# A stored sequence of steps in place of a planner's due times, in a kernel of attention and two feed-forward stages

## The chip, the cores and the metric

The kernel runs on one core of one Trainium2 chip. Times are microseconds (us) that the device takes for one execution, unless marked ns. The engines have short names here: PE is TensorE (matmuls), DVE is VectorE, ACT is ScalarE, POOL is GpSimd, and SP is SyncE, which issues all the DMAs of this kernel.

## What is computed

The reference has three stages in a row, on 4 batches of 576 tokens:

```python
scores = scale * q @ k.T                     # 4 batches, 8 heads, 576 x 64
# heads 0-3: a window of 32 tokens; heads 4-7: 128 tokens, every fourth
x = softmax(where(mask, scores, -1e9)) @ v   # as 2304 tokens x 512
h = x @ w_in                                 # 512 -> 1024
s = h * softmax(h)
x = (s - mean(s)) / sqrt(var(s) + 1e-6) * g_ln @ w_out    # 1024 -> 512
h = x @ w2_in                                # 512 -> 2048
out = softplus(h) @ w2_out                   # 2048 -> 512
```

Everything is float32 in and out. The kernel gets near float32 by splitting operands into a high and a low float16 part and adding three float16 products.

## The kernel before

The function describes its work as some 2,700 **steps**. A step has a name, the engines on which it may run (some can run on either ACT or DVE), a function that issues its instructions, the steps that must be over before it, and the buffers it uses, each from a pool with a few slots. There are 417 steps on PE, 343 on SP (the DMAs), and the rest are on ACT and DVE. Then `Plan.order` brings all steps into one sequence, and the last loop of the function issues them in that order, each on the engine that the plan gave it. An engine runs its instructions in the order in which they were issued, so this sequence is the whole schedule.

The names that come up below, in the order of the work:

- `ldN`, `pre..`, `w1i`, `w1o`, `w2i0` to `w2o3`: loads of a pair of attention blocks, the passes that find the scale of a batch, and the preparation of the weights in quarters (convert on DVE, square on ACT, a small matmul `...m` on PE that sums the squares, then a high half and a low half).
- `tqN`, `tkN`, `QKN`, `tpN`, `PVN`, `txN`: transposes, scores and values of attention pair N on PE. Pairs 0 to 9 are in float32 and use PE's transposes; pairs 10 to 27 are in float16 and use DMA transposes (`qT`, `kT`, `pT`, `xT`). With them go `cq`, `ck`, `cp`, `kh`, `ph`, `nr`, `xh` on ACT or DVE.
- `m1aT`, `m1bT`: the first matmul for token tile T (two steps of 12 matmuls); `m1n`, `m1h` and others are its normalisation.
- `yaJ`, `ybJ`: the matmul with `w_out` for a group J of 256 tokens.
- `hJ.P`, `oJ.P`: the last two matmuls (24 matmuls of 256 columns, 12 of 512); `sp`, `gh`, `gl` are softplus and the split between them. Groups 5 to 8 are done in pairs with seven products for eight, `P5..` and `P7..`.

`Plan.order` of the kernel before is a list scheduler. It keeps a clock of its own, a price for each step, and a latest time for each (`TABLE`, one number per step, in tenths of a us). Whenever an engine is free it takes the ready step with the earliest latest time whose buffers can be had, in the first free slot of each pool. A step that may run on either engine carries 509.77 us more on DVE's list (`SHY`). A step that needs ACT's other function table carries 20 us (`CLING`). When PE is free and has nothing ready in the first 400 us, the plan puts in a **fill**: one 128x512 matmul of the identity into a free PSUM slot, whose result nobody reads.

```python
            free = [f for f in self.fills if not f[0][0]]
            if idle_at["PE"] <= now + 1e-9 and now < self.FILL_END and free:
                idle_at["PE"] = self.pace(now, *self.FILL)
                ...
                out.append(min(free, key=lambda f: f[0][1])[1])
```

The sequence that comes out has 417 PE steps and 163 fills, 540 steps on ACT and 1,392 on DVE. ACT changes its table 53 times in it.

## Time and profile before

| | us |
|---|---|
| three runs | 704.28, 704.89, 707.59 |
| median | 704.89 |
| the profiled execution | 705.82 |
| its span, from the first to the last instruction | 704.1 |
| PE busy in the span | 680.0 |
| DVE busy | 569.9 |
| ACT busy | 464.7 |

### The profile page before, as it was taken

To read this page: it belongs to the slowest core of one execution; us is meant where nothing else is said; L and a number is where in the kernel's file an instruction comes from. 1 tells how busy PE (TensorE), PEld (TensorE's weight loads), DVE (VectorE), ACT (ScalarE), POOL (GpSimd) and SP (SyncE) were. 2 spreads that over 40 slices of the span, in tenths; PEclk is the share of its full clock that TensorE was granted. 3 is DMA by queue.
4 is the path that set the end of the run, shared out by engine and by line. 5 is a ranking of instruction groups with operands and counts; after the bars stand their busy time and mean duration, and the time that the engine had idled before them with its cause. 6 is when DMAs were issued, how large, how long until landed. Compare 5 with 4: busy or idle time off the path is not lost.

```text
span 704.1 us, 14232 instructions
## 1 busy us (share of the span) xinstructions
PE 680.0 (97%) x5244; PEld 465.6 (66%) x5244; DVE 569.9 (81%) x1668; ACT 464.7 (66%) x946; POOL 3.5 (1%) x22
## 2 busy tenths in 40 slices
PE   5999798999999999999999999999999999999997
PEld 3665556867766477778657767665867768777543
DVE  4799999999999887788989999898996487445342
ACT  5597997998977586778978878856655325123100
POOL 2000000000000000000000000000000000000000
PEclk9999779999999999999999999999999999999999
DMA  9977886669785448979887877453021110001001
GB/s 275 269 212 240 232 224 163 172 153 195 155 169 149 141 142 205 217 164 171 156 167 152 155 143 132 94 116 58 8 54 31 31 31 1 1 1 61 1 1 60
DMA packets 186773, 89.80 MB, mean 128 GB/s; under 512 B 157000, under 2 KB 174416, under 8 KB 186704
## 3 DMA queue, kind: packets, MB, share of 16 engines
q1 hardware_dynamic: 186704, 88.90, 54.4%
q8 instruction: 41, 0.67, 0.4%
q14 instruction: 28, 0.23, 0.1%
HBM read 54.53 MB, written 4.72 MB: 84 GB/s over the span
## 4 chain that ended last, share of the span: by engine, by line
PE 72%; DVE 13%; DMA 7%; ACT 4%; issue 2%; SPq 1%; ACTq 0%; DVEq 0%
PE ps_w L680 33%; PE bank L680 27%; PE bank L1678 10%; DVE W L671 2%; PE bank L686 2%; DMA pT<-p 2%; DVE E L671 1%; DMA rk<-in_k_dram 1%; DVE s L1250 1%; DVE st L1376 1%; DMA lnT<-hl 1%; DMA kT<-qk 1%; DVE qk L671 1%; SPq L689 1%; DMA W<-in_moe_w_out_dram 1%
## 5 line engine op out<-in xcount | busy, mean ns | idle before, releaser
L680 PE MATMUL ps_w<-W,g 128*128 128x512 f16 x864 | 194.2, 379 | 0.0
L680 PEld LDWEIGHTS <-W 128*128 128x128 f16 x1824 | 176.6, 98 | 24.9 <-issue 2.4
L680 PEld LDWEIGHTS <-g 128*128 128x128 f16 x864 | 83.3, 98 | 92.1
L680 PE MATMUL bank<-y,W 128*128 128x256 f16 x960 | 110.1, 273 | 1.6 <-ACT r L662 1.6
L680 PE MATMUL ps_w<-W,xr 128*128 128x512 f16 x432 | 99.5, 383 | 0.3 <-ACT xr L662 0.3
L680 PE MATMUL bank<-lnT,W 128*128 128x256 f16 x864 | 98.7, 273 | 0.0
L680 PEld LDWEIGHTS <-xr 128*128 128x128 f16 x432 | 41.9, 99 | 46.6 <-issue 2.0
L1853 ACT ACT_TABLE_LOAD x53 | 68.0, 1283 | 0.9
L662 ACT ACTIVATE s<-s 96x128 f32<-96x128 f32 (+3 forms) x144 | 43.8, 375 | 13.4 <-DVE s L668 11.8
L1678 PEld LDWEIGHTS <-W 128*128 128x128 f16 x480 | 46.9, 98 | 7.6
L671 DVE SCALAR_TENSOR_TENSOR g<-r,KR,g 128x512 f16<-128x512 f32 x66 | 49.2, 746 | 2.5 <-ACT g L662 0.4
L662 ACT ACTIVATE E<-E 128x768 f32<-128x768 f32 (+2 forms) x49 | 36.4, 744 | 14.8 <-DVE st L671 3.7
L666 DVE TENSOR_SCALAR g<-r,KR 128x512 f16<-128x512 f32 x35 | 16.9, 482 | 33.2 <-PE ps_w L680 30.1
L1250 DVE CUSTOM_DVE_ANT_0 s<-bank,band,bsc 96x128 f32<-96x128 f32 (+3 forms) x144 | 38.9, 322 | 1.3 <-PE bank L680 0.6
L662 ACT ACTIVATE r<-r,invT 128x512 f32<-128x512 f32 x19 | 13.4, 718 | 32.8 <-DVE r L674 32.8
L662 ACT ACTIVATE hl<-e,st 128x1024 f16<-128x1024 f32 x18 | 22.2, 1235 | 12.6 <-DMA lnT<-hl 8.2
L662 ACT ACTIVATE r<-bank,invC 128x512 f32<-128x512 f32 x40 | 27.3, 682 | 2.4 <-PE bank L680 1.6
L680 PEld LDWEIGHTS <-eye 128*128 128x128 bf16 (+2 forms) x183 | 18.4, 107 | 15.0 <-issue 4.1
L680 PEld LDWEIGHTS <-pT 128*96 128x96 f16 (+3 forms) x432 | 23.1, 124 | 7.2 <-DMA pT<-p 2.9
L662 ACT ACTIVATE e<-ps_w,st,bsc 128x1024 f32<-128x1024 f32 x16 | 19.3, 1205 | 11.6 <-DVE rs L666 4.5
L680 PE MATMUL ps_w<-eye 128*128 128x512 bf16 x101 | 26.9, 379 | 0.0
L671 DVE SCALAR_TENSOR_TENSOR E<-E 128x512 int32<-128x512 int32 x40 | 26.4, 681 | 0.1
(293 smaller groups left out, 1114.0 us busy)
## 6 DMA issues: line engine op xcount, KB each, us to landing
E<-in_moe_w_in_dram SPq DMA_DIRECT2D x17, 512.0 KB, 5.1
E<-in_moe_w_out_dram SPq DMA_DIRECT2D x17, 512.0 KB, 4.4
out_dram<-osb SPq DMA_DIRECT2D x18, 256.0 KB, 2.2
W<-in_moe_w_in_dram SPq DMA_DIRECT2D x7, 512.0 KB, 7.4
W<-in_moe_w_out_dram SPq DMA_DIRECT2D x7, 512.0 KB, 5.1
E<-in_v_dram SPq DMA_DIRECT2D x9, 384.0 KB, 3.8
E<-in_q_dram SPq DMA_DIRECT2D x9, 384.0 KB, 3.8
E<-in_k_dram SPq DMA_DIRECT2D x9, 384.0 KB, 4.1
```

The lines of the kernel that those rows point to most:

```text
L662: pin(nc.scalar.activation(out=out, in_=in_, func=func, **kw))
L666: pin(nc.vector.tensor_scalar(out=out, in0=in0, scalar1=s1, scalar2=None, op0=op0))
L671: pin(nc.vector.scalar_tensor_tensor(out=out, in0=in0, scalar=s, in1=in1, op0=op0, op1=op1, **kw))
L680: pin(nc.tensor.matmul(out, l, r, start=start, stop=stop))
L686: pin(nc.tensor.transpose(out, in_, eye32[:in_.shape[0], :in_.shape[0]]))
L689: pin(nc.sync.dma_start(out=out, in_=in_))
L1250: pin(nc.vector.tensor_tensor_reduce(out=sv()[:rows, h, :nk], in0=sb.t[:rows, h, :nk], in1=band[:rows, 48 - m:48 - m + nk], scale=sc[:rows ...
L1376: ({"DVE": (1.142, 0.14)}, lambda e: pin(nc.vector.tensor_reduce(out=col(0), in_=ph(), axis=AXX, op=ALU.max, negate=True)), [mb], [ps]),
L1678: pin(nc.tensor.matmul(ps.t[:, ff, :], at(w, cc, ff), yo.t[:, v, cc, :], start=start, stop=cc == 1 and x == 2, skip_group_check=True,))
L1853: pin(nc.scalar.preload_act_table_set(TABLES[tab]))
```

## The change

The steps, their functions, buffers and dependences stay as they are. The list scheduler, its prices and the table of latest times go. In their place stand two stored lists. `ORDER` names the steps one after the other; a number below zero is a fill, and a number at or above the count of steps (2,692) means that the step runs on DVE where it could also run on ACT. `SLOTS` names the slot for each buffer, in the order in which the buffers are first used. `order` only reads them and asserts that dependences and slots are kept:

```diff
-    SHY = 509.77
-    WIN, KEEP, HOLD = 3.4133, 3.0, 3.2
-    FILL = (0.235, 0.48)
...
-    CLING = 20.0
...
     def order(self):
 
-        for o in reversed(self.ops):
-            late = min((s.late for s in o.succ), default=1e9)
...
+        out, over, n = [], set(), len(self.ops)
+        slots = iter(self.slots)
+        for x in self.stored:
+            if x < 0:
+                place, bank = self.fills[-1 - x]
+                assert not place[0]
+                out.append(bank)
+                continue
+            o = self.ops[x % n]
+            assert o not in over and all(a in over for a in o.after), o.name
+            o.on = next(iter(o.opts)) if len(o.opts) == 1 else "DVE" if x >= n else "ACT"
             for b in o.uses:
...
+                if b.slot is None:
+                    assert not b.pool.fifo or b.n == b.pool.next, o.name
+                    b.slot = b.pool.slots[next(slots)]
...
-    TABLE = (
...
+    ORDER = (
+        65, 66, 247, 248, 278, 277, 0, 13, -2, -2, -2, 250, 252, 2943, 3, 2945, 14, 67, 69, -2, -2, 280, 254, 281,
+        1, 255, 266, 267, 256, 15, 16, 4, 249, 68, -5, -5, -5, -5, -5, -5, -5, 257, 5, 279, 282, 6, 28, 308, 18,
...
+    SLOTS = (
+        0, 0, 0, 1, 1, 0, 0, 0, 1, 0, 1, 0, 0, 1, 0, 0, 1, 2, 1, 0, 0, 1, 0, 1, 0, 2, 0, 3, 0, 0, 0, 1, 0, 1, 0, 0,
...
-    lanes = Pool("lanes", [None] * P.LANES, fifo=False)
```

Set beside the sequence before, the stored one holds:

| | before | stored |
|---|---|---|
| fills | 163 | 142 |
| steps on ACT | 540 | 588 |
| steps on DVE | 1,392 | 1,344 |
| changes of ACT's table | 53 | 43 |
| steps that change from DVE to ACT, from ACT to DVE | | 109, 61 |
| PE steps at another place in PE's own order | | 264 of 417 |
| DMAs at another place in SP's own order | | 285 of 343 |

Where the fills stand, and the PE steps around them, at the places that come up later (`[6F]` is six fills):

```
before  [18 fills so far] tk1 [7F] tq1 pre0m ...            58 fills ahead of w1im, 95 of m1a0
        tp8.1 [6F] PV7.0 PV7.1 PV8.0 PV8.1 [7F] tx7.0 [4F] tx7.1 [7F] tx8.0 [3F] ya0.1     133 ahead of ya0.1
        w2i3m [4F] PV13.0 [1F] ... m1b6 m1a7 m1b7 [12F] m1a8 w2o3m m1b8                    163
stored  [3F] tq0 tk0 ... tp0.0 tk1 tp0.1 ...                58 fills ahead of w1im, 88 of m1a0
        tp8.0 [5F] PV7.0 PV7.1 tp8.1 [4F] tx7.0 [6F] tx7.1 PV8.0 PV8.1 [2F] ya0.1          113 ahead of ya0.1
        [1F] w2i3m [3F] PV13.0 [1F] ... [1F] ... m1b6 m1a7 m1b7 [4F] m1a8 w2o3m m1b8       142
```

After `m1a8` neither sequence has a fill.

## Rows read from the trace of the kernel before

**Rows 1.** The page: busy time by engine.

```profile
PE 680.0 (97%) x5244; PEld 465.6 (66%) x5244; DVE 569.9 (81%) x1668; ACT 464.7 (66%) x946; POOL 3.5 (1%) x22
```

**Rows 2.** Windows by stage: stretch, its length, busy time (instructions), clock, DMA.

```profile
0.00:35.20 35.20, 28.04 (x199) 16.72 (x200) 21.14 (x54) 19.91 (x62) 3.52 (x22) 0.95 0.97 272
35.20:134.30 99.10, 91.73 (x693) 61.34 (x692) 97.23 (x283) 88.25 (x255) 0.00 (x0) 0.91 0.72 207
134.30:222.80 88.50, 88.13 (x713) 62.48 (x711) 88.09 (x283) 79.91 (x159) 0.00 (x0) 1.00 0.80 167
222.80:243.90 21.10, 20.82 (x116) 9.89 (x115) 19.54 (x47) 10.18 (x18) 0.00 (x0) 1.00 0.51 150
243.90:456.50 212.60, 208.27 (x1824) 152.45 (x1824) 184.88 (x673) 174.71 (x313) 0.00 (x0) 1.00 0.77 158
456.50:699.40 242.90, 242.90 (x1709) 162.76 (x1707) 158.25 (x333) 91.10 (x142) 0.00 (x0) 1.00 0.14 31
```

**Rows 3.** Timeline of PE: fills at either clock, an early wait; start, length, what.

```profile
11.02 2.54 PE L680 MATMUL bank<-eye 128*128 128x512 bf16 x11
...
16.34 0.47 PE L686 MATMUL bank<-eye,rk 80*128 80x80 f32 x4 [2.77 <-DMA rk<-in_k_dram]
...
87.29 2.34 PE L680 MATMUL bank<-eye 128*128 128x512 bf16 x5
...
238.61 2.75 PE L680 MATMUL bank<-eye 128*128 128x512 bf16 x12
```

**Rows 4.** Lines by form: kinds that move, and the table load.

```profile
L1853 ACT ACT_TABLE_LOAD x53 | 68.0, 1283 | 0.9
...
L662 ACT ACTIVATE xf<-bank,rs 80x64 f32<-80x64 f32 x52 | 11.9, 313 | 2.1 <-DVE rs L677 2.1
...
L1376 DVE TENSOR_REDUCE st<-ps_w 128x1 f32<-128x1024 f32 x18 | 21.9, 1217 | 1.8 <-PE ps_w L680 1.8
...
L662 ACT ACTIVATE e<-e,st 128x1024 f32<-128x1024 f32 x8 | 9.9, 1233 | 1.2 <-DVE st L668 1.1
...
L668 DVE TENSOR_SCALAR e<-e,st 128x1024 f32<-128x1024 f32 x10 | 8.1, 809 | 0.2
...
L674 DVE TENSOR_TENSOR xf<-bank,rs 80x256 f32<-80x256 f32 x19 | 7.9, 417 | 0.2
```

**Rows 5.** Timeline of DVE at 198 us: starts and lengths of neighbours.

```profile
198.26 0.74 DVE L666 TENSOR_SCALAR osb<-ps_w,invD 128x512 f32<-128x512 f32 x1
198.92 0.14 DVE L668 TENSOR_SCALAR s2o<-s2o 128x1 int32<-128x1 int32 x1
```

**Rows 6.** Waits of PE from 243.9 us on: total, times, longest.

```profile
PE bank L680 <- DMA pT<-p: 1.9, 2, 1.5
PE bank L680 <- ACT r L662: 1.2, 2, 0.9
PE bank L680 <- DMA kT<-qk: 0.8, 1, 0.8
PE bank L680 <- DVE s L1250: 0.4, 1, 0.4
```

**Rows 7.** Timeline at the end.

```profile
699.63 0.69 ACT L662 ACTIVATE osb<-ps_w,iD 128x512 f32<-128x512 f32 x1 [4.49 <-PE ps_w L680]
700.36 0.75 DVE L666 TENSOR_SCALAR osb<-ps_w,iD 128x512 f32<-128x512 f32 x1 [4.43 <-ACT osb L662]
```

**Rows 8.** Windows around the stretch in which PE's clock falls.

```profile
74.00:78.00 4.00, 2.12 (x32) 1.84 (x28) 4.00 (x11) 4.00 (x12) 0.00 (x0) 1.00 0.76 250
78.00:94.00 16.00, 13.46 (x69) 9.25 (x70) 15.26 (x39) 16.00 (x45) 0.00 (x0) 0.50 0.95 252
94.00:98.00 4.00, 3.29 (x18) 1.57 (x17) 4.00 (x18) 4.00 (x15) 0.00 (x0) 0.85 1.13 295
```

**Rows 9.** Timeline of PE: a block of 12 matmuls at the low clock, and at the full one.

```profile
92.46 4.11 PE L680 MATMUL ps_w<-W,xr 128*128 128x512 f16 x12
...
241.29 2.75 PE L680 MATMUL ps_w<-W,xr 128*128 128x512 f16 x12
```

## The prediction

> **What bounds the kernel now.** I read the page first. PE is busy 97% of the span [rows 1], but that counts fills and the tails of overlapping matmuls, so it doesn't say where time can be won. The windows by stage do [rows 2]. The last column groups to look at are PE, DVE and ACT against the length of each stretch.

> - To 35.2 us the first pairs and weights come in. No engine is full (PE 28.04 of 35.20, and most of that is fills); the DMA engines are at 0.97 of their share.
> - From 35.2 to 222.8 us DVE is full: 97.23 of 99.10 and 88.09 of 88.50, which leaves 2.3 us idle in 187.6. In the first of these stretches PE is not short of time, since a good part of its 91.73 is fills. In the second PE is full too (88.13), nearly without fills.
> - From 222.8 to 243.9 PE spends 16 fills, 12 of them in a row [rows 3], until the last weight quarter is ready.
> - From 243.9 to 456.5 PE waits only 4.3 us (208.27 of 212.60), and from there to 699.4 not at all (242.90 of 242.90). The last 4.7 us are the last copies and the output.

> So the end is the moment at which the last weight quarter's sum of squares, `w2o3m` at 243.9, goes through, plus a fixed mass of matmuls, plus 4.3 us of waits, plus 4.7. What the change is worth is read from two places: how much earlier `w2o3m` comes, for which DVE's queue is the measure, and how many of the 4.3 us go.

> **DVE's queue ahead of `w2o3m`.** I set the two sequences beside each other and took the steps that stand on DVE up to the last one on which `w2o3m` depends: 593 before, 579 in the stored one. The difference is made of four parts, priced by [rows 4].

> - 20 steps leave for ACT: two `m1n` at 0.809 us, and 18 others of which the commonest is `nr` at 0.417. 2 x 0.809 + 18 x 0.417 = 9.1 us less.
> - 7 steps come from ACT, among them three copies out of PSUM. Bounds: 7 x 0.417 = 2.9, or, at the 0.74 of a 128x512 step out of PSUM [rows 5], 5.2. I take 3.8, nearer to the first because the copies have 320 columns and not 512.
> - The maximum of token tile 7 (1.217) with its small follower goes behind: 1.3 us less. A small step (0.2) comes ahead.

> That is -9.1 + 3.8 - 1.3 + 0.2 = -6.4. But neighbours on DVE overlap: a step of 0.74 us is followed by the next after 0.66 [rows 5]. 14 steps fewer are 14 such overlaps of 0.08 fewer, 1.1 us. Net **-5.3 us**. The same count at `h0.0` (134.3 us) gives -4.7, so most of it is won in the first of DVE's full stretches.

> **The fills say the same.** 21 fills fewer: 12 in a row took 2.75 us and 11 took 2.54 [rows 3], 0.21 each, so 4.4 us. At the low clock five took 2.34, near 0.45 each, which would make 9.4. Fills stand where the planner expected PE to wait, so a shorter wait and fewer fills are one gain and not two. 4.4 and 5.3 agree; I take 5.3, as the measure of the engine that is full, and keep 9.4 as the far end and nothing as the near end.

> **What I cost at nothing.**

> - ACT's extra work ahead of `w2o3m`: five more `nr` net, each four instructions of 0.313, make 6.3; two `m1n` at 1.233 make 2.5; six short steps net at about 0.5 make 3. With overlaps that is some 9 us. It hides in ACT's idle time, 8.6 us in the second full stretch and 10.9 in the one behind it [rows 2]. Without that cover it is a rival below.
> - 10 table loads fewer, 12.8 us of ACT at 1.283 each [rows 4]. Both sequences have 10 changes of table ahead of `w2o3m`, so all ten are saved later, where ACT is busy 174.71 of 212.60 and 91.10 of 242.90 [rows 2]. No gain; if ACT set PE's pace there, up to 1.2 us of waits hang on ACT [rows 6].
> - SP's order. The k load of pair 1 goes from 11th to 4th place, which ends a wait of 2.77 us [rows 3]; the last piece of `w_in` goes from 20th to 24th, behind four more loads of 128 KB, which at 272 GB/s [rows 2] is 1.9 us. Both lie ahead of `w1im`, which has 58 fills before it in either sequence. I take them as cancelling, and keep -2.8 and +1.9 as bounds.
> - Slots. They choose among buffers of equal speed; a bad choice would show as a wait and belongs to the rivals.
> - The end. In both sequences the last `o` is followed by one copy on ACT, one on DVE behind it [rows 7], and the output. 4.7 us stay.

> **The 4.3 us of late waits** are six [rows 6]. Two are for DMA transposes of the probabilities (1.9 us, ahead of `PV19.0` and `PV24.0`), which DVE feeds. By the stored sequence DVE has 13.0 and 14.2 us less ahead of these, and PE 7.8 and 5.6 less: DVE gains on PE by 5.2 and 8.6, more than the 1.5 and 0.4 waited. They go: **-1.9 us**. The other four (2.4 us) keep their distance and stay.

> **Sum.** 704.1 - 5.3 - 1.9 = 696.9 us of span. The profiled execution was 705.82, 1.7 more than its span, and 0.9 above the median of 704.89. I take the 7.2 off the median: **697.7 us**.

> **Rivals.**

> - *ACT becomes the bound* (the other side). Place: 134.3 to 222.8. ACT is busy 79.91 of 88.50 there [rows 2]; ten steps come over to it inside the stretch and none leave, 6.8 us by the kinds above, which makes 86.7. If ACT's 8.6 us of waiting are for the same inputs as before and stay, the stretch takes 95.3, 6.8 more. Should ACT (0.5 us more ahead of `h0.0`) also hold back the 4.7 won until there, the end is 704.89 + 6.8 + 0.5 - 1.9 = 710.3. It decides for slower once more than 3.7 us of the 8.6 stay. For it: ACT is then the fuller engine. Against it: these waits were mostly for DVE's results, and DVE comes earlier; and 12 fills (2.75) behind it are cover. Chance 0.10, of which 0.07 end above 708.4.
> - *PE's clock falls more often.* [...] Chance 0.08, half to each end. [...]
> - *New late waits.* From 456.5 on PE has nothing to win and its order is changed all the same. In the first set of seven products the third was the seventh step of PE behind the seventh product and is now the fourth, with two additions on DVE to be done between. If the stored sequence fits the plan's times closer than the chip's, the 4.3 us of waits double instead of shrinking: 704.89 - 5.3 + 4.3 = 703.9. For it: 264 of 417 PE steps stand elsewhere. Against it: DVE has 10 to 20 us less ahead of PE from 400 us on. Chance 0.10.
> - *The fills were only cover.* PE waits as long as before with fewer fills in the gap; only the 1.9 come: 703.0. For it: ahead of `ya0.1` the fills fall from 133 to 113, while DVE's queue ahead of it, counted as above, does not shrink. Chance 0.06.
> - More than forecast: waits under low-clock fills go too (9.4) and the early 2.8: below 691.5, chance 0.04.

> **How the numbers follow.** The forecast has 0.62, with a range of its own of 692 to 701. From 691.5 to 705 leaves out the 0.04 below and about 0.11 above. A difference under 0.5% (3.5 us) can hardly be told from no change. Faster: 0.62 + 0.04 + 0.04 (the clock's near end) = 0.70. Slower: 0.07 + 0.04 = 0.11. The same: 0.10 + 0.06 + 0.03 = 0.19.

> **What would show it.** Right: `w2o3m` near 238.6 us, the run of fills ahead of it 4 and not 12; DVE still full from 35 to about 218; late waits near 2.4 us with those for DMA `pT` gone; 43 table loads less one or none; 4.7 us at the end. Wrong: ACT full and DVE idle between 130 and 218 (the first rival); more than 16 us of granted clock at 0.50 (the second); waits of PE after 456 us (the third); `w2o3m` still at 243 with gaps in place of fills (the fourth).

## The result, and the profile after

The changed kernel takes 697.87 us (median of 4 runs, 697.51 to 698.44), beside 705.78 for the kernel before in 4 runs of the same session: a ratio of 0.9888, interval 0.986 to 0.9915. The forecast was 697.7 us. The profiled execution took 698.44, its span 696.5.

The page's busy line of the changed kernel, to be set against [rows 1]:

```profile
PE 675.2 (97%) x5223; PEld 463.9 (67%) x5223; DVE 556.0 (80%) x1619; ACT 480.9 (69%) x1015; POOL 3.5 (1%) x22
```

Its windows between the same steps as in [rows 2] (columns as there; `h0.0` now starts at 128.5, `w2i3m` at 218.3, `w2o3m` at 238.2):

```profile
0.00:32.10 32.10, 27.89 (x201) 17.14 (x202) 22.18 (x56) 19.27 (x63) 3.54 (x22) 1.00 0.91 255
32.10:128.50 96.40, 87.84 (x673) 59.21 (x672) 92.47 (x268) 88.07 (x257) 0.00 (x0) 0.91 0.86 222
128.50:218.30 89.80, 89.30 (x716) 62.75 (x715) 88.77 (x284) 86.25 (x179) 0.00 (x0) 1.00 0.78 172
218.30:238.20 19.90, 18.89 (x108) 9.23 (x108) 18.62 (x43) 11.93 (x26) 0.00 (x0) 1.00 0.52 146
238.20:448.80 210.60, 208.08 (x1826) 152.66 (x1825) 179.08 (x649) 176.20 (x341) 0.00 (x0) 1.00 0.80 160
448.80:691.80 243.00, 243.00 (x1709) 162.95 (x1707) 154.17 (x322) 98.50 (x155) 0.00 (x0) 1.00 0.14 31
```

Up to `w2o3m` DVE is busy for 22.18 + 92.47 + 88.77 + 18.62 = 222.0 us, which leaves 16.2 idle. Before it was 226.0 of 243.9, 17.9 idle [rows 2]. So the 5.7 us by which `w2o3m` comes earlier are 4.0 of work and 1.7 of idle time. ACT is busy 86.25 of 89.80 in the third stretch and DVE is still full there; the stretch itself is 1.3 us longer than before. Behind 448.8 nothing has changed: 243.00 of 243.00.

The run of fills ahead of the last weight quarter, in PE's timeline (start, length, what): four, where [rows 3] had twelve.

```profile
234.79 1.03 PE L552 MATMUL bank<-eye 128*128 128x512 bf16 x4
235.66 2.75 PE L552 MATMUL ps_w<-W,xr 128*128 128x512 f16 x12
```

PE's waits from 238.2 us on, the counterpart of [rows 6] (total, times, longest). They sum to 2.4 us, as forecast, but are not the four that were to be left:

```profile
PE bank L552 <- DMA pT<-p: 1.0, 1, 1.0
PE bank L552 <- DMA qT<-qk: 0.5, 1, 0.5
PE bank L552 <- DVE xf L546: 0.5, 1, 0.5
PE bank L552 <- ACT xf L534: 0.4, 1, 0.4
```

So the two profiles put the gain of 7.6 us of span (704.1 to 696.5) in two places: 5.7 ahead of `w2o3m` and 1.9 behind it, where 460.2 us became 458.3 and the waits of PE fell from 4.3 to 2.4.

The table load among the lines by form, ten fewer than in [rows 4], and the end of the timeline, which answers to [rows 7] (696.5 - 691.8 is again 4.7):

```profile
L1718 ACT ACT_TABLE_LOAD x43 | 55.2, 1283 | 0.7
```

```profile
692.04 0.69 ACT L534 ACTIVATE osb<-ps_w,iD 128x512 f32<-128x512 f32 x1 [8.95 <-issue]
...
692.76 0.75 DVE L538 TENSOR_SCALAR osb<-ps_w,iD 128x512 f32<-128x512 f32 x1 [6.69 <-ACT osb L534]
```

PE's clock, in windows of 4 us (compare [rows 8]). The drop to 0.50 comes at about 75 us instead of 78 and lasts no longer, about 17 us in either. In the window ahead of it PE had 2.11 us of work in 4, and in the one in which it comes 0.98:

```profile
70.00:74.00 4.00, 2.11 (x28) 1.65 (x24) 4.00 (x12) 4.00 (x13) 0.00 (x0) 1.00 0.90 276
74.00:78.00 4.00, 0.98 (x9) 0.84 (x9) 4.00 (x10) 2.84 (x8) 0.00 (x0) 0.69 0.98 238
78.00:82.00 4.00, 3.11 (x21) 2.72 (x20) 2.80 (x8) 4.00 (x13) 0.00 (x0) 0.50 0.73 212
...
90.00:94.00 4.00, 4.00 (x18) 1.97 (x16) 3.81 (x13) 4.00 (x10) 0.00 (x0) 0.67 0.99 289
```

Where the lead arises is seen from the starts of PE's steps: `m1a0` 53.6 before and 48.9 after, `h0.0` 134.3 and 128.5, `w2i3m` 222.8 and 218.3, `w2o3m` 243.9 and 238.2, the last `o` 696.8 and 689.2. Of the early lead 3.1 us are there where the second window begins (32.1 for 35.2), and 4.8 at `m1a0`, early in the first stretch in which DVE was full.

### The profile page after: what moved, and what is told of

It is laid out like the page before. It is cut to its first block, busy times and chain, and to the rows that moved or that the text cites. A ratio compares the mean times of both kernels' runs of the same rounds, so it can differ in the third digit from the quotient of the medians.

```text
span 696.5 us, 14184 instructions
## 1 busy us (share of the span) xinstructions
PE 675.2 (97%) x5223; PEld 463.9 (67%) x5223; DVE 556.0 (80%) x1619; ACT 480.9 (69%) x1015; POOL 3.5 (1%) x22
## 2 busy tenths in 40 slices
DMA packets 186773, 89.80 MB, mean 129 GB/s; under 512 B 157000, under 2 KB 174416, under 8 KB 186704
## 4 chain that ended last, share of the span: by engine, by line
PE 69%; DVE 12%; DMA 10%; ACT 4%; issue 3%; SPq 1%; ACTq 0%; DVEq 0%
PE ps_w L552 31%; PE bank L552 26%; PE bank L1550 11%; DMA xd<-x 2%; DVE E L543 2%; DMA E<-in_v_dram 2%; DMA qT<-qk 1%; DMA pT<-p 1%; DVE W L543 1%; PE bank L558 1%; DVE s L1122 1%; DMA W<-in_moe_w_out_dram 1%; ACT E L534 1%; DMA rv<-in_v_dram 1%; DMA rq<-in_q_dram 1%
## 5 line engine op out<-in xcount | busy, mean ns | idle before, releaser
L543 DVE SCALAR_TENSOR_TENSOR g<-r,KR,g 128x512 f16<-128x512 f32 x68 | 50.3, 744 | 15.2 <-ACT g L534 14.2
L534 ACT ACTIVATE E<-E 128x768 f32<-128x768 f32 (+3 forms) x51 | 37.9, 744 | 15.7 <-DVE E L543 8.8
L534 ACT ACTIVATE xf<-bank,rs 80x64 f32<-80x64 f32 (+1 forms) x128 | 29.3, 314 | 7.2 <-DVE rs L549 4.8
L552 PE MATMUL ps_w<-eye 128*128 128x512 bf16 x108 | 31.4, 407 | 0.7 <-DVE e L543 0.7
L534 ACT ACTIVATE g<-r,KR 128x512 f16<-128x512 f32 x35 | 24.9, 715 | 6.6 <-PE ps_w L552 6.3
L552 PEld LDWEIGHTS <-eye 128*128 128x128 bf16 (+2 forms) x162 | 16.5, 111 | 15.8 <-POOL eye L611 4.0
```

The costliest lines, as they stand in the source:

```text
L534: pin(nc.scalar.activation(out=out, in_=in_, func=func, **kw))
L543: pin(nc.vector.scalar_tensor_tensor(out=out, in0=in0, scalar=s, in1=in1, op0=op0, op1=op1, **kw))
L552: pin(nc.tensor.matmul(out, l, r, start=start, stop=stop))
```

## The experiments

Each was timed beside the kernel before, which had a median of 704.84, 704.47 and 705.03 us in the three sessions (e1 to e4, e5 to e8, e9 to e12). Three kinds of edit were made: sequences cut at a step (the one list up to it, the steps that are left in the order of the other), engines put back (a number at or above 2,692 is a step on DVE), and fills. Buffers keep the slots of the part from which they come. One table for all; "work" and "idle" are DVE's, up to the start of `w2o3m`:

| | us | ratio, interval | `m1a0` | `w2o3m` | work | idle |
|---|---|---|---|---|---|---|
| before | 705.78 | 1 | 53.6 | 243.9 | 226.0 | 17.9 |
| after | 697.87 | 0.9888, 0.986 to 0.9915 | 48.9 | 238.2 | 222.0 | 16.2 |
| e1 new head | 704.34 | 0.9996, 0.9979 to 1.0014 | 49.0 | 244.5 | 227.9 | 16.6 |
| e2 old head | 703.17 | 0.9975, 0.995 to 0.9999 | 55.9 | 244.6 | 221.6 | 23.0 |
| e3 new early, old late | 696.64 | 0.9879, 0.9855 to 0.9903 | 48.4 | 238.1 | 222.2 | 15.9 |
| e4 new order, old engines | 729.42 | 1.0341, 1.0315 to 1.0367 | 54.9 | 246.7 | 226.5 | 20.2 |
| e5 before, fewer fills | 707.07 | 1.0038, 1.0009 to 1.0067 | 55.6 | 251.6 | | |
| e6 after, more fills | 697.91 | 0.9905, 0.9877 to 0.9933 | 48.8 | 240.2 | | |
| e7 before, new early engines | 712.51 | 1.0118, 1.008 to 1.0155 | 53.7 | 252.5 | 223.0 | 29.5 |
| e8 after, old early engines | 707.03 | 1.0045, 1.0017 to 1.0074 | 53.6 | 245.0 | 226.4 | 18.6 |
| e9 old engines to `m1a0` | 703.34 | 0.9986, 0.9959 to 1.0013 | 53.9 | 241.3 | 221.5 | 19.8 |
| e10 old engines from there | 702.04 | 0.9956, 0.9935 to 0.9976 | 48.4 | 243.4 | 227.4 | 16.0 |
| e11 old early, new late | 705.26 | 0.9995, 0.9975 to 1.0015 | 53.7 | 244.0 | | |
| e12 e3 with cover | 697.93 | 0.9903, 0.9871 to 0.9936 | 49.3 | 239.9 | | |

### The sequence, cut at a step (e1, e2, e3, e11)

**e1**, the stored sequence up to `m1a0` (340) and then that of before:

```diff
         ... 434, 86, 340,
-        435, 100, 442, 87, 113, 443, 101, 88, 341, 392,
+        1164, 506, 562, 113, 87, 453, 88, 104, 392, 143, 3085,
...
```

> The stored sequence up to its first m1a0 (88 fills), then the sequence of before for all other steps, with its engines and slots and its 68 later fills. In the new kernel's profile m1a0 starts at 48.9 us, 4.8 earlier than before. Theory of the head (the new kernel wins most of its early gain ahead of m1a0, because DVE and ACT get work sooner in the first 35 us, and a full DVE carries that on): about 4 to 5 us faster than before, near 701. Theory of the queue (the gain is that DVE has 5.3 us less work ahead of w2o3m, as the prediction had it): at most the 1.5 us of the 7 fills, near 704.

**e2**, the opposite cut at the same step:

```diff
         ... 440, 88, 340,
-        104, 392, 385, 441, 143, 434, 3085, 100, 435,
+        441, 385, 434, 435, 100, 442, 443, 101, 341, 392,
...
```

> The sequence of before up to its first m1a0 (95 fills), then the stored sequence for all other steps with its engines, slots and 54 later fills. Theory of the head: 4 to 5 us slower than the new kernel, near 702.5, since the shorter queue later only takes back what DVE now idles. Theory of the queue: near 699, as the queue ahead of w2o3m is still some 4 us shorter.

**e3**, the stored sequence up to `w2o3m` (854) and then that of before:

```diff
         ... 1356, 667, 854,
-        855, 856, 857, 858, 859, 860, 861, 668, 1295,
+        1357, 668, 669, 1431, 855, 856, 1295, 857, 671,
...
```

> The stored sequence up to w2o3m (142 fills, none later), then the order, engines and slots of before. By the prediction's split the part from 243.9 us on is worth 1.9 us: 1.9 slower than the new kernel, near 699.8, with waits of PE behind w2o3m of some 4.3 us. Rival (the late order is worth nothing, all is early): within 0.5 us of the new kernel.

**e11**, the opposite cut at `w2o3m`:

```diff
         ... 668, 669, 854,
-        1431, 855, 856, 1295, 857, 671, 858, 859,
+        855, 856, 857, 858, 859, 860, 861, 1295, 862,
...
```

> The sequence of before up to w2o3m and the stored one behind it, with its engines and its ten table loads fewer. The forecast gave the late part 1.9 us: 704.5 - 1.9 = 702.6. Rival, taken from the run with the opposite cut, which was at least as fast as the new kernel with the late part of before: the late part is worth nothing, 704 to 705.

The head alone wins nothing, 704.34 us, and what follows it alone 1.7 of 704.84. Together they win 7 to 8. So neither theory is enough by itself: e1 came out at the number of the queue's, e2 nearer to that of the head's. In e1 PE is at `m1a0` 4.6 us earlier and has lost that again by `w2o3m`; in e2 DVE has as little work as in the changed kernel, and idles 6.8 us longer, some 2 of them because the old head of this execution was itself late (55.9 at `m1a0`; see the last section). The windows up to `w2o3m` of e1, then of e2:

```profile
0.00:244.50 244.50, 225.94 (x1707) 148.56 (x1707) 227.89 (x665) 196.56 (x487) 3.53 (x22) 0.97 0.77 196
```

```profile
0.00:244.60 244.60, 228.52 (x1700) 151.70 (x1701) 221.63 (x646) 208.10 (x526) 3.54 (x22) 0.94 0.79 196
```

e3 and e11 place the gain in time: all that can be measured comes from the order and the engines ahead of `w2o3m`. With the late part of before, its 53 table loads with it, e3 is at 696.64 at least as fast as the changed kernel. The new late part alone gives 705.26 beside 705.03. Late waits of PE in e3, which has the late order of before, then in e11, which has the new one:

```profile
PE bank L559 <- DMA pT<-p: 1.6, 1, 1.6
PE bank L559 <- DVE E L577: 0.3, 1, 0.3
```

```profile
PE bank L560 <- ACT r L542: 0.9, 1, 0.9
PE bank L560 <- DMA qT<-qk: 0.5, 1, 0.5
PE bank L560 <- ACT xf L542: 0.3, 1, 0.3
PE bank L560 <- DMA kT<-qk: 0.2, 1, 0.2
```

That is 1.9 us in either. Over all profiles the late waits of PE sum to 1.2 to 4.3 us with the late order of before (4.3 before, 4.1 in e1, 2.6 in e7, 2.3 in e12, 1.9 in e3, 1.2 in e5) and to 1.0 to 3.2 with the new one. (e4, whose late engines are others, is left out.) With the old late order they are long where the early part gives no lead (before, e1) and short where the engines come to `w2o3m` with a lead (e3, e12) or PE comes late (e5, e7). So a lead is enough to shorten them, without the new late order. The profile of e11 has the new order, no lead and 2.4 us less of them than before, so in a single execution the order can be enough too. But this execution took 703.42 us, 1.8 less than the median of e11, and the median has no gain.

### Engines put back (e4, e8, e9, e10), and engines without the order (e7)

**e4**, all 170 steps that changed engine on their old one; **e8**, the 27 of them that lie ahead of `w2o3m`. The numbers are those of single steps in the list:

```diff
-        250, 252, 2943, 3, 2945, 14,
+        250, 252, 251, 3, 253, 14,
...
```

> The stored sequence in its order, with its fills and slots, but each of the 170 steps that changed between DVE and ACT on the engine that it had before. Ahead of w2o3m that puts 5.1 us back on DVE (20 steps back, 7 away). Theory of the queue: w2o3m is 4 to 5 us later than in the new kernel, 702 to 703 in all. Theory of the head: most steps that moved ahead of m1a0 are few, so m1a0 stays near 49 to 50 and the total is within 2 us of the new kernel.

> The stored sequence in its order, with these 27 early steps alone put back on the engines of before. In the run with all 170 put back w2o3m came 8.5 us later than in the new kernel and the rest lost 15 more. If the early steps account for the first part alone, w2o3m is near 246 and the total is some 8 us above the new kernel, near 706. If the late loss came from the late start, it comes here too, near 715 or more.

**e9**, only the 12 ahead of `m1a0` (seven go back to ACT, five to DVE; some of them):

```diff
-        2943     # cq0
+        251
-        303      # nr1.1c
+        2995
-        2753     # w1i.6h
+        61
```

> The new kernel with 12 of the 27 early engine changes undone: those ahead of m1a0 in the stored sequence (seven copies and conversions go back from VectorE to ScalarE, five from ScalarE to VectorE). Theory one, the head is won by order and engines together: m1a0 goes back from 48.9 to 53.6, where it stood with all 27 undone and with the kernel before, VectorE is idle some 5 us more in the head, this lead is not made up afterwards, and the time is 697.9 + 4.7 = 702.6 or a little less. Theory two, only VectorE's work counts ahead of w2o3m: the swaps put two steps net on VectorE, undoing them takes some 0.7 us of durations off it, m1a0 is late but w2o3m is within 1 us of 238.2, and the time is 697 to 698.5.

**e10**, only the 15 between `m1a0` and `w2o3m` (all back to DVE; some of them):

```diff
-        393      # nr3.1c
+        3085
-        417      # m1n1
+        3109
-        1240     # nr11.1c
+        3932
```

> The new kernel with the other 15 of the 27 early engine changes undone: those between m1a0 and w2o3m, all from VectorE to ScalarE, go back to VectorE. Theory one, VectorE's queue: m1a0 stays at 48.9, VectorE's busy time behind it rises by 4 to 7 us, w2o3m comes at 242 to 245 and the time is 702 to 704. Theory two, the head's lead decides and these steps find idle time on VectorE: w2o3m within 1 us of 238.2, time 697 to 699. With the run before: if both put back together cost 9.2 us (707.0) and the two apart cost less in sum, the two parts depend on each other.

**e7**, the sequence of before with the same 27 on their new engines:

```diff
-        251      # cq0
+        2943
-        3085     # nr3.1c
+        393
...
```

> The sequence of before with its fills, and only the 27 steps ahead of w2o3m that change engine put where the new kernel has them (20 to ACT, 7 to DVE); all later ones stay. Theory of the queue (DVE's work sets the time): DVE has 4.2 us less ahead of w2o3m, so about 4 us faster, near 701. Rival (a step moved to ACT without its place being changed waits in ACT's queue, or makes others wait, and DVE idles as much as it saves): no faster than before, 704 to 708.

With the stored order and the old early engines nothing is left of the gain (e8, 707.03), and the old order with the new early engines loses (e7, 712.51). The order is worth something only with the engines for which it was made, and the other way about. e9 and e10 cut e8's loss in two: against 697.87, which is of another session, it is 9.2 us, theirs are 5.5 and 4.2. Their windows up to `w2o3m`, e9 and then e10, beside the 222.0 and 16.2 of the changed kernel:

```profile
0.00:241.30 241.30, 224.29 (x1695) 148.47 (x1696) 221.47 (x646) 207.58 (x526) 3.52 (x22) 0.96 0.79 199
```

```profile
0.00:243.40 243.40, 226.72 (x1693) 150.06 (x1694) 227.36 (x664) 196.85 (x486) 3.52 (x22) 0.95 0.80 197
```

In e10 DVE has 5.3 us more of work and in sum no more idle time: this is the step that the forecast counted. But its profile holds more than this step. PE waits 2.2 us for ACT ahead of 103.2 (0.2 at this place in the changed kernel), the clock falls a second time, and DVE stands 3.6 us for PE:

```profile
104.00:112.00 8.00, 8.00 (x43) 5.15 (x42) 4.88 (x17) 6.04 (x21) 0.00 (x0) 0.57 0.62 134
```

This execution took 704.84 us, 2.8 more than the median of e10. Of the twelve executions of e10 the three slowest (704.0 to 706.2) have the three lowest mean clocks (0.979 to 0.982; the others 0.984 to 0.990). So in most of them `w2o3m` will be nearer 240.6 than 243.4 (an estimate: 243.4 less the 2.8).

In e9 DVE has 0.5 less work and 3.6 more idle time. DVE's waits in the first 54 us show where, in the changed kernel and then in e9:

```profile
DVE qT L538 <- PE bank L558: 5.1, 1, 5.1
DVE W L540 <- DMA E<-in_moe_w_in_dram: 1.6, 1, 1.6
```

```profile
DVE W L547 <- DMA E<-in_moe_w_in_dram: 7.9, 1, 7.9
DVE s L1020 <- PE bank L559: 2.5, 3, 1.2
DVE xf L553 <- PE bank L565: 1.6, 1, 1.6
```

In e9 DVE's first work of any length is a weight piece, for whose transfer it stands 7.9 us. In the changed kernel the copies `cq0` and `ck0` of the first pair run in that time, at 6.15 and 6.84. Up to `m1a0` DVE works hardly longer in the changed kernel than in e9 (38.56 and 37.87 us): it does work whose data are there, where it stood still. The engine swaps in the head put two steps net on DVE and still win 3.0 us at `w2o3m`.

e7 has the opposite fault. DVE's work falls by 3.0 us and its idle time rises by 11.6. Its window up to `w2o3m`, and its longest waits behind `m1a0`:

```profile
0.00:252.50 252.50, 229.27 (x1715) 149.80 (x1715) 222.96 (x649) 207.61 (x521) 3.54 (x22) 0.97 0.75 190
```

```profile
DVE tmp L668 <- PE bank L560: 2.8, 1, 2.8
DVE x L554 <- ACT x L542: 1.9, 1, 1.9
DVE tmp L746 <- PE bank L560: 1.6, 3, 0.8
DVE x L578 <- ACT xf L542: 1.5, 1, 1.5
DVE E L548 <- DMA E<-in_moe_w_in_dram: 1.2, 1, 1.2
DVE hl L554 <- ACT hl L542: 1.2, 1, 1.2
```

Three of these six are for ACT. In the same stretch of the kernel before, DVE has only two waits that the profile lists, 1.2 us for PE and 0.7 for a transfer. By what ended these waits, steps went to places in ACT's queue that come too late, and DVE, which takes its steps in the order of the sequence too, stands behind them; no run moves such a step by itself. e4 has the like late, where the other 143 steps went back. At 729.42 us it is far from both of its numbers: `w2o3m` comes at 246.7, and what follows takes 481.3 us where the changed kernel takes 458.3. PE's waits from 246.7 us on begin with

```profile
PE bank L559 <- ACT xf L541: 6.6, 2, 4.9
PE bank L559 <- DVE s L1129: 3.6, 5, 1.4
PE ps_w L559 <- DVE e L550: 2.4, 2, 1.8
```

### Fills and the clock (e5, e6, e12)

**e5**, the sequence of before with 21 fills fewer (8 of the 12 ahead of `m1a8`, 10 between `tp8.1` and `ya0.1`, 3 ahead of `tp5.1`); **e6**, the changed kernel with 21 fills more at these places:

```diff
         1356, -1, 848,
-        -1, -1, -1, 667, -1, 1293, -1, -1, -1, -1, -1, -1, 850, 1430,
+        -1, -1, 667, 1293, 850, 1430,
...
```

```diff
-        -1, -1, -1, -1, 1430, 848,
+        -1, -1, -1, -1, -1, -1, -1, -1, -1, -1, -1, -1, 1430, 848,
...
```

> The sequence of before with 21 of its 163 fills taken out and nothing else: 8 of the 12 ahead of m1a8, 10 between tp8.1 and ya0.1 (7 ahead of tx8.0, 3 ahead of ya0.1), 3 ahead of tp5.1. That leaves 142, as in the new kernel. Theory that fills are only cover (DVE and ACT set the time of this stretch, PE then waits where the fills stood): within 1 us of before, and PE idle for some 4 us more. Rival (each fill is 0.21 us on the path, as the prediction's second count had it): 4.4 us faster, near 700.5. Rival of the clock: slower by one or more low-clock blocks at 1.4 us each.

> The stored sequence with 21 fills put in at the same three places: 8 more ahead of m1a8, 10 ahead of ya0.1, 3 ahead of tp5.1; 163 in all. Fills as work on the path: up to 4.5 us slower than the new kernel, near 702. Fills as cover: PE waits only 1.5 us between ya0.1 and w2o3m in the new kernel, so what 21 fills add there is more than it waits; with DVE idle some 3 us there too, 1 to 3 us slower, near 700.

**e12**, e3 with 17 fills more around its two early waits of PE (6 ahead of `PV5.1`, 3 of `tx5.0`, 8 of `tq8`). Behind these e3's granted clock is 0.50 in each window of 4 us from 74 to 90; the question was whether this stretch, up to `h0.0`, takes its time from the low clock or from DVE and its data:

```diff
         ... 362,
+        -4, -4, -4, -4, -4, -4, -4, -4,
         881, 882,
...
```

> [...] Theory two, VectorE and the data set the pace in that stretch: the clock rises or not, h0.0 stays within 0.7 us of 127.9, time 696 to 698.

21 fills more cost nothing (697.91 us, where both theories had some loss); 21 fewer win nothing and cost a little (707.07). In e6 `w2o3m` is 2.0 us later than in the changed kernel, and the end is not: the late waits are 1.0 us in place of 2.4, and the rest of the delay is made up behind `w2o3m` as well, where no run resolves it.

In e5 the clock is low for about 20.4 us between `m1a0` and `w2i1m`, before for 17.0 (reckoned from the granted clock in windows of 4 and 2 us, with 0.50 as the low clock), and at other places. The first low stretch, from 82 us, is shorter: 10.2 us. A second lies at 98 to 106 us, a third at 122 to 126:

```profile
98.00:102.00 4.00, 2.89 (x16) 2.39 (x17) 3.63 (x12) 3.90 (x10) 0.00 (x0) 0.61 0.62 192
102.00:106.00 4.00, 4.00 (x11) 1.55 (x10) 2.25 (x9) 2.65 (x5) 0.00 (x0) 0.54 0.41 120
...
122.00:124.00 2.00, 2.00 (x14) 1.57 (x14) 2.00 (x6) 0.85 (x6) 0.00 (x0) 0.69 0.40 120
124.00:126.00 2.00, 2.00 (x12) 1.38 (x11) 2.00 (x7) 1.45 (x3) 0.00 (x0) 0.50 0.00 0
```

Before, the clock is at 1.00 in all of these. The second stretch follows a wait of PE of 2.7 us for DVE (0.7 before), and no fill was taken out near it; a block of 12 matmuls takes 4.93 us in it. The third lies behind the ten fills taken out ahead of `ya0.1`: PE now waits 1.9 and 0.5 us there, and the 48 matmuls that follow take 1.7 us more. They are, before and then in e5:

```profile
117.37 5.40 PE L680 MATMUL bank<-lnT,W 128*128 128x256 f16 x48
```

```profile
121.91 7.07 PE L559 MATMUL bank<-lnT,W 128*128 128x256 f16 x48 [0.54 <-DVE st L547]
```

By `w2i1m` (122.6 us before) e5 is 6.2 us behind, of which 2.0 were there at `m1a0`, ahead of every fill taken out. Of the other 4.2, the 1.7 at the third stretch are a little more than one of the expectation's low-clock blocks (1.4, from the 4.11 and 2.75 of [rows 9]). That the fills taken out made the third stretch is seen in this one execution alone; that they made the second too is not shown. Both are paid by the kernel before with fills taken out, not by the changed one, and this execution, 710.35 us, is 3.3 above the median of e5.

In e12 the low clock is shorter than in e3, about 13.6 us for 20.5 (reckoned in the same way), but the time is not. It comes in two pieces, 74 to 82 and 86 to 98 us:

```profile
74.00:78.00 4.00, 1.76 (x7) 0.89 (x8) 4.00 (x10) 2.82 (x7) 0.00 (x0) 0.81 1.04 239
78.00:82.00 4.00, 4.00 (x26) 2.50 (x25) 0.50 (x1) 1.27 (x5) 0.00 (x0) 0.77 0.23 89
82.00:86.00 4.00, 2.12 (x18) 1.47 (x17) 3.52 (x9) 4.00 (x13) 0.00 (x0) 1.00 0.79 174
...
90.00:94.00 4.00, 3.67 (x16) 1.99 (x15) 4.00 (x11) 4.00 (x16) 0.00 (x0) 0.50 0.95 331
```

From 78 to 82 PE is full, partly with fills, and DVE works 0.50 of 4.00 us: it waits 3.5 us for a result of ACT, which by PE's order depends on matmuls that stand behind the fills. `h0.0` comes at 131.0, 3.1 later than in e3, which is outside the 0.7 us expected; the time, 697.93 us, lies in the 696 to 698. So the shorter low clock won no time here.

## Why the forecast held, step by step

- **The size.** 697.7 forecast, 697.87 measured. The profiles also split it nearly as forecast: 5.7 us ahead of `w2o3m` (5.3 forecast) and 1.9 behind it (1.9). But neither part came about in the way that was worked out, as the points below show, so that the sum is this close is partly luck.
- **"DVE's queue ahead of `w2o3m`", -5.3.** Right as the mechanism of the larger part. DVE's work up to there fell by 4.0 us. The 15 steps that leave DVE behind `m1a0` are worth 5.3 of it by e10, the swaps in the head take 0.5 back by e9 and the order 0.4 by e8 (226.4 beside 226.0); that makes 4.4, and the last 0.4 is not resolved. The working priced work only. That idle time on DVE can be filled by another engine assignment was missing from it: e9 shows 3.6 us of it.
- **"So most of it is won in the first of DVE's full stretches"** was wrong. Of the 5.8 us at `h0.0` 3.1 are won ahead of that stretch, and the lead stands at 4.8 early in it, at `m1a0`. But it is kept only where the 15 steps leave DVE behind it: in e10 a lead of 5.2 at `m1a0` shrinks to 0.5 at `w2o3m`, of which some 2.8 may be the second fall of the clock in that execution. Counting one queue to its end gave nearly the right sum for a wrong place.
- **SP's order, "I take them as cancelling".** Not tried by itself, but e8 and e9 have SP's new order with the old engines in the head. There `tk1`, the first step of PE on the k load of pair 1, starts 2.9 and 2.6 us earlier than before, and `w1im` only 0.8 and 0.5. So at nothing the term was nearly right; the 3.2 us at `w1im` in the changed kernel need the new engines too.
- **"The fills say the same", 4.4 us.** One gain and not two, right: e5 and e6 show that fills by themselves have no price here (21 fewer 707.07 beside 704.47, 21 more 697.91 beside 697.87). For the same reason they were no second measure of the gain, and that 4.4 and 5.3 agree shows nothing.
- **ACT's extra work hidden.** Right: 86.25 us busy in the third stretch, 86.7 forecast, with 3.6 idle where 8.6 were; ahead of `w2o3m` ACT has 7.3 us more work, some 9 forecast. (The break-even of the rival left out its own 0.5 us: it is 3.2 of the 8.6, not 3.7.) The rival itself is nearest to what e7 shows, 8.0 us slower than the median beside it, when the engines change and the order does not.
- **Ten table loads, no gain.** Right: e3 has all 53 and is not slower (696.64 beside 697.87).
- **The late waits, "They go: -1.9 us".** The size came, the working failed. 2.4 us are left as forecast, but one `pT` wait is still there, the four that were to stay are gone, and three others have come. The working read DVE's gain on PE at two places out of the new sequence. e3 has the old late order and shorter waits still (1.9 us, and 457.2 us from `w2o3m` to the end), e11 the new one, equally short waits in its profile and no gain in its median. The waits depend at least in part on how far the engines are at `w2o3m`; how much of the 1.9 us the late order makes stays open.
- **The clock.** The drop lasts no longer (about 17 us in either), and between `tp8` and `ya0.1`, where the fills are fewer, the granted clock of the changed kernel is 1.00 (98 to 126 us). No run shows the two ends between which the 0.08 of this rival is halved. What the runs show is e5, the old sequence with fills taken out at that place: a clock of 0.69 and 0.50 there, and 7.07 us for 48 matmuls that took 5.40 before. The end stays at 4.7 us, as taken. Slots were not tried by themselves; in the kernel before, the 960 matmuls of 128x256 that write `bank` from `y` and `W` all take 269 to 278 ns.

## What to carry to other kernels

Where two in-order engines share work, the time of a late step is the work ahead of it on the full engine plus that engine's idle time; count both, because a move from one engine to the other changes both, and with the wrong order it wins work and loses more in waits (e7: 3.0 us less work, 11.6 more idle, so `w2o3m` at 223.0 + 29.5 = 252.5 us instead of 243.9). Judge an order and its engine assignment together: the head alone, the rest alone, the order alone and the engines alone each won 0 to 1.7 us here or lost, and all together 7 to 8. A wait of one or two us behind the bound is a poor price: here the late waits went from 4.3 us down to 1.0 with what happened ahead of them.

## What the runs showed that I had not expected

The head of the sequence of before reached `m1a0` at 53.6, 53.7, 55.6 and 55.9 us in four profiled executions (before, e11, e5, e2) with the same instructions up to there; the stored head at 48.4 to 49.3 in six. The clock differs: behind PE's wait for the k load of pair 1 it is low for about 3.4, 3.4, 10.2 and 6.8 us in these four between 14 and 28 us (reckoned as above; before, the windows of 2 us from 16 on have 0.67, 0.50 and 0.98), and in the stored heads not at all (1.00 to 32 us in the changed kernel). That is not what wins the head, since e7, e8 and e9 have no low clock there either and reach `m1a0` at 53.7, 53.6 and 53.9. The timed runs of the kernel before spread over 701 to 711 us in the last session, those of the changed kernel over 697.5 to 698.4 in four. In e5, e8, e9 and e10 too the slower executions have the lower mean clock (in e8 nine at 704.8 to 707.8 us with 0.986 to 0.988, three at 711.4 to 712.5 with 0.976 to 0.978; in e9 nine at 701.6 to 703.7 with 0.984 to 0.988, three at 706.8 to 708.9 with 0.975 to 0.981; in e5 seven at 703.0 to 707.6 with 0.982 to 0.988, five at 707.6 to 711.1 with 0.977 to 0.981), so differences of one to three us between these may be the clock's in part. And a delay of `w2o3m` is not paid in full: it came 7.6 us later in e5 and 2.0 later in e6 than in the kernel before and in the changed one, and the last `o` 4.5 later and 0.5 earlier.
